# Induced-set attention with a SwiGLU network: shared load buffers and one visit of seven chunks for each attention product

## The chip, the cores and the metric

The kernel runs on one core of one Trainium2 chip. The metric is device time in microseconds (us) of one execution, the median of three runs. Engines are named as the profile names them: PE is TensorE, DVE is VectorE, ACT is ScalarE, POOL is GpSimd, SP is the sync engine, which issues the transfers.

## The reference

Four batches of 12416 tokens of 128 channels go through two attentions: 32 inducing vectors attend to the tokens, and the tokens attend to the result. What comes out (49664 tokens) goes through a gated network with 1536 hidden units.

```
def mab(q, kv):
    s = scale * (q @ kv.transpose(0, 2, 1))
    s = s - s.max(-1, keepdims=True)
    a = np.exp(s)
    a /= a.sum(-1, keepdims=True) + 1e-09
    return a @ kv
h = mab(I, x)                 # I: (4, 32, 128), x: (4, 12416, 128)
attn_out = mab(x, h)
...
g = x @ w_gate                # x: attn_out as (49664, 128)
silu = g * (1.0 / (1.0 + np.exp(-g)))
val = x @ w_val
return (silu * val @ w_out)
```

## The kernel before

**The network.** It takes nearly all of the time. The tokens of a batch make 25 columns (the code's list COLS), the hidden units 12 tiles of 128, so a batch has 300 *slots*, one for a column and a tile. In a slot the program issues, in this order of the queues:

- the *front*: two matmuls on PE, gate (L694) and value (L695), each into a PSUM buffer of the pool ps_gv. The pool has six buffers, so three pairs. The weights of this product contain the attention's result, spread over a tile called stack.
- the silu of the gate on ACT (L700), and the product of silu and value on DVE (L708). For tiles 1, 5 and 9 (DVE_TILES) the product stays in PSUM (gv); the others go into a pool of five h buffers.
- the cast of the product to h_hi on ACT (L716) and the rest h_lo on POOL, for tiles 1, 5 and 9 on DVE (both L718). Tile 11 is cast on DVE (L211). These steps, called now(w) in the code, are held back by one to three slots in a list called wait.
- the *back*: three matmuls on PE (L737, L738, L739) that add the tile's share to the output o. A back belongs to a front of 6 to 11 slots earlier; the list pend holds the fronts whose back is to come, and the number called ahead says how many it may hold. Behind the 12th back of a column DVE copies o out (L748) and SP sends it (L749).

**The attention.** It goes in *chunks*: 97 blocks of 128 tokens in seven chunks of 14 (the last 13). Batch 0's runs first, by tables of tokens (START, SECOND, FIRST). The attention of batches 1, 2 and 3 is laid into the slots of the batch before by the function plan, which gives every step a slot (add) from a dictionary of distances: PA for the *first planned batch*, PB for the *two later batches*. The main loop issues the steps that are due behind the front of the slot and ahead of its back. For one planned batch:

- load_xt brings a chunk's columns from memory into one of four buffers (xtp), load_xn its rows into one of three (xnp), both through SP.
- s1, the *scores*: matmuls of 14 blocks a chunk (L275), four chunks at one slot and three at another, seven chunks in two visits. A *visit* is a stretch in which PE leaves the network for the attention. DVE transposes the scores and takes their maximum.
- the *burst*, at one slot called e1: ACT computes all the exponentials (L307). It needs another table for this and loads silu's table back behind it. At a burst every cast that is held back goes to DVE, and ahead falls to 6, so that several backs follow at once. DVE makes a transposed tile of each chunk of exponentials, eT (L313), in a pool of four buffers.
- hacc, the *weighted sum*: matmuls of the eT tiles and the rows (L323), in three visits of three, two and two chunks, each two visits some slots apart. The first visit also sums up (h_a, L331), DVE takes the reciprocal (h_r, L335) and the normalized part (h_b); behind each later visit h_s adds that part (L344). Then h_c prepares the result.
- s2, the *second scores* of all tokens against the result: again four chunks and three (L275 too), with four more loads of columns for the first visit and the other three kept from the scores (the list S2O). DVE transposes them (L445) and takes the maximum (s2_max, L453), POOL subtracts it (s2_sub, L457).
- the second burst, e2, and then for each of six column groups: sum, reciprocal, normalization (L471, POOL), transpose to aT (L475, DVE), a_hi and a_lo (L484, POOL), and transfers to the tile stack.

A visit of steps that carry a set acc is held until the next back in pend is of none of the tiles 11, 0, 1 and 2, since it uses the PSUM buffer o between two columns.

Counted in slots of the batch that it lies in, the first planned batch has its scores at 86 and 103, the burst at 131, the weighted sums at 134, 146 and 158, the second scores at 185 and 199 and the second burst at 208. For the two later batches these are 47 and 67, 84, then 87, 96 and 102, then 127 and 138, and 149.

Of the kernel before, what the change touches and what calls it, by code (L numbers as in the profile page):

```python
# [111 lines left out]
def induced_set_attention_then_swiglu(ctx: ExitStack, tc: tile.TileContext, xt, xn, ind, wgv, wo, out):  # L112
# [103 lines left out]
    def attention(b, one, xn0=None, xt0=None):  # L216
# [88 lines left out]
        def exp1_part(q, to=None, g=0):  # L305
            sp = slice(span(q).start, span(q if to is None else to).stop)
            nc.scalar.activation(out=st.s[:, sp], in_=st.s[:, sp], func=AF.Exp, bias=st.negmax[:, g:g + 1], scale=1.0,  # L307
                                 accum_out=st.sum1[:, q:q + 1])
# [253 lines left out]
    def plan(st, p):  # L562
# [24 lines left out]
        for q in range(NXN):
            add(e1 - p["LN"][0] + p["LN"][1] * q, "load_xn", q)
            add(e1, "exp1_part", q)
            add(e1, "eT", q)  # L590
            add(e1 + p["HA"][q], "hacc", q, (0, NXN - 1))
        add(e1 + p["HA"][NXN - 1], "h_a")
        add(e1 + p["HA"][NXN - 1] + 1, "h_r")
        add(e1 + p["HA"][NXN - 1] + 1, "h_b")
        add(e1, "exp1_part", NXN, NCH - 1)
        for q in range(NXN, NCH):
            k = NXN + (q - NXN | 1)
            at = e1 + p["HB"][0] + p["HB"][1] * (k - NXN)
            add(max(at - p["HC"][0] - k + q, e1 + 1 + (p["HB"][0] + p["HB"][1] if q == NCH - 1 else p["HA"][0])), "load_xn", q)
            add(at - p["HC"][1] + 1 - k + q, "eT", q)  # L600
            add(at, "hacc", q, (k - 1, k))
        add(at + 1, "h_s")
        hn = at + p["HD"]
        add(hn, "h_c")
        for i, q in enumerate(S2O):
            k = i % NXT
            at = hn + 4 + p["H2"] * (NXT - 1) if i < NXT else hn + p["H2"] * (NCH - 1)
# [261 lines left out]
```

## Time and profile before

| what | value |
|---|---|
| median of three runs | 1376.85 us (1376.74 to 1377.32) |
| the profiled execution | 1376.59 us |
| its span | 1374.8 us |
| PE busy | 1366.1 us, 99% of the span, 7459 instructions |
| ACT busy | 1245.7 us, 91% |
| DVE busy | 1195.4 us, 87% |
| POOL busy | 1179.8 us, 86% |
| transfer queue q1 | 117.90 MB, 26.3% of 16 engines |

The span is what lies between the first and the last instruction of the profiled execution. An engine's busy time is the sum of its instructions; the matmuls of PE are pipelined, so that their modelled durations overlap and starts say more than durations. The clock that PE was granted is full (a 9) in all 40 slices of the page. Three other engines are busy for 86 to 91%, so none of them has much in hand. A row of the timeline gives the start, the time, the engine, the line, the operation, output<-input with sizes, and how many were joined (x3); in square brackets stands the idle time ahead of it and who ended that.

### The profile page before, as it was taken

What the parts mean: (1) busy time and instruction counts of PE and PEld (TensorE: products, weight loads), DVE (VectorE), ACT (ScalarE), POOL (GpSimd) and SP (SyncE); (2) the same over time, 40 slices, a digit from 0 to 9 for tenths busy, and PEclk for the clock granted to TensorE, in tenths of its full rate; (3) what the DMA queues carried; (4) which work ended last, traced back from release to release, by engine and by line L of the source; (5) the groups of instructions that cost most, each with busy time, mean ns of one, the idle gap of its engine ahead of it and who ended that gap; (6) DMA issues with size and microseconds to landing.
All of it is one profiled execution on the core that took longest, in us unless ns stands there. A gap on an engine that the chain in (4) does not pass through costs nothing.

```text
span 1374.8 us, 25215 instructions
## 1 busy us (share of the span) xinstructions
PE 1366.1 (99%) x7459; PEld 1183.8 (86%) x7459; DVE 1195.4 (87%) x2088; ACT 1245.7 (91%) x2380; POOL 1179.8 (86%) x994
## 2 busy tenths in 40 slices
PE   9999999999999999999999999999999999999998
PEld 6578788889988887899998888789999888889998
DVE  6899879998988889898898888988888888888887
ACT  4989898889998887999999889799999999999998
POOL 1689878989988878899899878889989989989987
PEclk9999999999999999999999999999999999999999
DMA  9234433312144243221123522321111111111110
GB/s 370 81 96 133 160 104 114 119 56 71 38 130 160 94 143 112 67 62 37 44 72 119 192 80 95 123 73 52 44 38 45 39 47 39 39 46 38 43 44 22
DMA packets 50680, 119.49 MB, mean 87 GB/s; under 512 B 11376, under 2 KB 28272, under 8 KB 50544
## 3 DMA queue, kind: packets, MB, share of 16 engines
q1 hardware_dynamic: 50544, 117.90, 26.3%
q8 instruction: 59, 0.97, 0.3%
q14 instruction: 77, 0.63, 0.2%
HBM read 62.54 MB, written 25.43 MB: 64 GB/s over the span
## 4 chain that ended last, share of the span: by engine, by line
PE 97%; ACT 1%; DMA 1%; DVE 1%; issue 0%; SPq 0%; DVEq 0%
PE o L737 18%; PE gv L694 18%; PE gv L695 18%; PE o L738 18%; PE o L739 18%; PE gv L275 2%; PE o L323 1%; PE o L275 1%; DMA xt_sb<-xt 1%; PE o L734 0%; ACT silu L700 0%; PE gv L424 0%; PE gv L267 0%; ACT xn_sb L184 0%; DVE eT L313 0%
## 5 line engine op out<-in xcount | busy, mean ns | idle before, releaser
L718 POOL TENSOR_TENSOR h_lo<-h,h_hi 128x512 fp32r<-128x512 f32 (+1 forms) x889 | 1088.6, 1250 | 147.7 <-ACT h_hi L716 104.7
L700 ACT ACTIVATE silu<-gv 128x512 f32<-128x512 f32 (+1 forms) x1200 | 704.8, 589 | 95.5 <-PE gv L694 69.9
L708 DVE TENSOR_TENSOR h<-gv,silu 128x512 f32<-128x512 f32 (+1 forms) x891 | 590.9, 669 | 90.5 <-PE o L738 50.7
L716 ACT CAST h_hi<-h 128x512 fp32r<-128x512 f32 (+1 forms) x778 | 468.9, 603 | 0.8 <-DVE h L708 0.8
L694 PE MATMUL gv<-stack,tw 128*128 128x512 f32 (+1 forms) x1200 | 452.7, 377 | 1.3 <-DVE stack L544 1.0
L695 PE MATMUL gv<-stack,tw 128*128 128x512 f32 (+1 forms) x1200 | 448.2, 374 | 0.0
L737 PE MATMUL o<-h_hi,wo_lo 128*128 128x512 f32 (+1 forms) x1188 | 445.6, 375 | 0.0
L739 PE MATMUL o<-h_lo,wo_hi 128*128 128x512 f32 (+1 forms) x1188 | 443.2, 373 | 0.0
L738 PE MATMUL o<-h_hi,wo_hi 128*128 128x512 f32 (+1 forms) x1188 | 443.2, 373 | 0.0
L708 DVE TENSOR_TENSOR gv<-gv,silu 128x512 f32<-128x512 f32 (+1 forms) x297 | 201.5, 678 | 66.0 <-PE o L738 46.0
L694 PEld LDWEIGHTS gv<-stack,tw 128*128 128x128 f32 x1200 | 227.0, 189 | 33.9 <-ACT tw L416 3.0
L737 PEld LDWEIGHTS o<-h_hi,wo_lo 128*128 128x128 f32 x1188 | 224.8, 189 | 33.4 <-issue 10.6
L695 PEld LDWEIGHTS gv<-stack,tw 128*128 128x128 f32 x1200 | 227.0, 189 | 28.0 <-ACT silu L700 1.6
L739 PEld LDWEIGHTS o<-h_lo,wo_hi 128*128 128x128 f32 x1188 | 224.8, 189 | 24.3 <-POOL h_lo L718 0.3
L738 PEld LDWEIGHTS o<-h_hi,wo_hi 128*128 128x128 f32 x1188 | 224.8, 189 | 23.2
L718 DVE TENSOR_TENSOR h_lo<-gv,h_hi 128x512 fp32r<-128x512 f32 (+1 forms) x297 | 197.6, 665 | 0.8
L716 ACT CAST h_hi<-gv 128x512 fp32r<-128x512 f32 (+1 forms) x295 | 168.8, 572 | 10.1 <-DVE gv L708 8.4
L211 DVE TENSOR_REDUCE h_hi<-h 128x512 fp32r<-128x512 f32 (+1 forms) x113 | 73.7, 661 | 0.0
L748 DVE COPY ob<-o 128x512 f32<-128x512 f32 (+1 forms) x99 | 65.8, 665 | 0.2 <-PE o L739 0.2
L484 POOL TENSOR_TENSOR a_lo<-aT,a_hi 128x480 fp32r<-128x480 f32 (+2 forms) x26 | 29.9, 1151 | 0.0
L196 POOL TENSOR_TENSOR wgv_sb<-s_all 128x512 int32<-128x512 int32 x2 | 2.9, 1487 | 28.4 <-ACT s_all L184 28.4
L471 POOL TENSOR_TENSOR s_all<-s_all,sm 128x512 f32<-128x512 f32 (+2 forms) x27 | 26.1, 966 | 0.0
(156 smaller groups left out, 480.2 us busy)
## 6 DMA issues: line engine op xcount, KB each, us to landing
xt_sb<-xt SPq DMA_DIRECT2D x32, 896.0 KB, 5.1
xn_sb<-xn SPq DMA_DIRECT2D x18, 896.0 KB, 6.1
out<-ob SPq DMA_DIRECT2D x52, 256.0 KB, 2.0
out<-ob SPq DMA_DIRECT2D x48, 240.0 KB, 2.0
stack<-a_hi SPq DMA_DIRECT2D x96, 64.0 KB, 2.0
stack<-a_lo SPq DMA_DIRECT2D x96, 64.0 KB, 2.0
stack<-a_hi SPq DMA_DIRECT2D x96, 60.0 KB, 2.0
stack<-a_lo SPq DMA_DIRECT2D x96, 60.0 KB, 2.0
```

Of the source, the lines that this page charges most:

```text
L211: nc.vector.tensor_reduce(out=out, in_=in_.unsqueeze(2), op=ALU.max, axis=AX.X)
L275: nc.tensor.matmul(out=ps[32 * j:32 * j + 32, 32 * (lo - b0):32 * (hi - b0)], lhsT=lhsT, rhs=st.xt[q][:, lo - CH0[q]:hi - CH0[q], j, :], s ...
L694: nc.tensor.matmul(out=u.g[:, :n], lhsT=st.w[:, wcol(0, t)], rhs=rhs, start=True, stop=True)
L695: nc.tensor.matmul(out=u.v[:, :n], lhsT=st.w[:, wcol(1, t)], rhs=rhs, start=True, stop=True)
L700: nc.scalar.activation(out=u.s[:, :u.n], in_=u.g[:, :u.n], func=AF.Silu)
L708: nc.vector.tensor_mul(out=u.h[:, :n], in0=u.v[:, :n], in1=u.s[:, :n])
L716: u.cast(out=u.hi[:, :n], in_=u.h[:, :n])
L718: eng.tensor_sub(out=u.lo[:, :n], in0=u.h[:, :n], in1=u.hi[:, :n].bitcast(F32))
L737: nc.tensor.matmul(out=o[:, :n], lhsT=wo_lo[:, ws], rhs=hi, start=(t == 0), stop=False)
L738: nc.tensor.matmul(out=o[:, :n], lhsT=wo_hi[:, ws], rhs=hi, start=False, stop=False)
L739: nc.tensor.matmul(out=o[:, :n], lhsT=wo_hi[:, ws], rhs=lo, start=False, stop=(t == NT - 1))
L748: (nc.scalar.copy if u.last else nc.vector.tensor_copy)(out=ob[:, :n], in_=o[:, :n])
```

## The change

For the planned batches both pools of load buffers serve both kinds of load: chunks 0 to 3 use the four buffers of xtp, chunks 4 to 6 the three of xnp, for columns and for rows, one after the other. So each kind of load can have all seven chunks in place, and scores, weighted sums and second scores become one visit of seven chunks each. The columns are loaded twice for all chunks (14 loads a batch instead of 10). The partial sums h_s are gone, and h_b is done once. The four instructions of the burst take other groups of chunks (EXPS). Four eT tiles are made at the burst, the other three at the weighted sum's slot, in turn with its matmuls. At the slots of scores and second scores the held tiles of DVE_TILES are finished first. The PSUM buffer rule (acc), the ramps and everything of the network are as before. Lines of the kernel after the change are a few off: L686 and L687 are the front, L692 silu, L700 the product, L710 h_lo, L729 to L731 the back.

In slots, the first planned batch now has its scores at 103, the burst at 131, the weighted sum at 134, the second scores at 170 and the second burst at 191. The two later batches: 67, 87, planned 90 and by the acc rule at 93, then 115 and 141.

```diff
-S2O = list(range(NCH - NXT, NCH)) + list(range(NCH - NXT))
 NXN = 3
+EXPS = [(0, 0), (1, 1), (2, 3), (4, 6)]
+NET = 4
...
-PA = dict(LX=(51, 5), S1=(61, 7), MX=7, E1=21, LN=(27, 4), HA=(3, 3, 3), HB=(9, 6), HC=(11, 4), HD=5, H2=6, E2=5, PR=(0, 3), PQ=2)
-PB = dict(LX=(0, 9), S1=(25, 7), MX=6, E1=11, LN=(28, 4), HA=(3, 3, 3), HB=(9, 3), HC=(10, 4), HD=6, H2=5, E2=7, PR=(0, 3), PQ=1)
+PA = dict(LX=(51, 5), S1=103, MX=7, E1=21, LN=3, HA=3, HD=5, LS=4, S2=6, E2=5, PR=(0, 3), PQ=2)
+PB = dict(LX=(0, 9), S1=67, MX=6, E1=14, LN=3, HA=3, HD=6, LS=3, S2=6, E2=5, PR=(0, 3), PQ=1)
...
-                else:
-                    st.xt[q] = xtp.tile([P, max(CH), NG, 32], F32, name="xt_sb")
+                elif xn0 is not None or q < NXT:
+                    st.xt[q] = xtp.tile([P, max(CH), NG, 32], F32, name="xt_sb")
+                else:
+                    st.xt[q] = xnp.tile([P, max(CH), C], F32, name="xn_sb").rearrange("p i (j r) -> p i j r", r=32)
...
-                if xn0 is None or q < NXN:
+                if xn0 is None and q < NXT:
+                    t = xtp.tile([P, max(CH), NG, 32], F32, name="xt_sb").rearrange("p i j r -> p i (j r)")
+                elif xn0 is None or q < NXN:
                     t = xnp.tile([P, max(CH), C], F32, name="xn_sb")
...
-            if q == group[1] and 0 < group[0] < NXN + 1:
-                h_s()
...
-        def h_s():
-            nc.vector.scalar_tensor_tensor(out=st.hn, in0=st.hps[:, 0:C], scalar=st.r, in1=st.hn, op0=ALU.mult, op1=ALU.add)
...
-            add(v1 if q < NXT else last, "s1", q, q not in (0, NXT))
...
+            add(p["LX"][0] + p["LX"][1] * q, "load_xt", q)
+            add(v1, "s1", q, q != 0)
...
+        for q in range(NCH):
+            add(v1 + 1 + p["LN"] * q, "load_xn", q)
+        for i, (q, to) in enumerate(EXPS):
+            add(e1, "exp1_part", q, to, 0, i)
+        va = e1 + p["HA"]
+        for q in range(NCH):
+            add(e1 if q < NET else va, "eT", q)
+            if q >= NET - 1:
+                add(va, "hacc", q - NET + 1, (0, NCH - 1))
+        for q in range(NCH - NET + 1, NCH):
+            add(va, "hacc", q, (0, NCH - 1))
+        add(va, "h_a"), add(va, "h_r"), add(va, "h_b")
+        add(va + p["HD"], "h_c")
+        for q in range(NCH):
+            add(va + 1 + p["LS"] * q, "load_xt", q)
+        v2 = va + 1 + p["LS"] * (NCH - 1) + p["S2"]
+        for q in range(NCH):
+            add(v2, "s2", *blocks(q), q != 0)
+            add(v2 + 1 + 2 * q, "s2_max", *blocks(q))
+            add(v2 + 3 + 3 * q, "s2_sub", *blocks(q))
+        e2 = v2 + 3 + 3 * (NCH - 1) + p["E2"]
...
-                    if step == "h_s":
+                    if step == "h_b":
                         a.hb = slot
+                    if step in ("s1", "s2"):
+                        for w in [w for w in wait if w.t in DVE_TILES]:
+                            now(w)
```

How the order of the queues moves is shown at three places.

**First place**: DVE's queue at the burst of the first planned batch and behind it. h_hi rows are the casts that the burst gives to DVE, s_all holds the exponentials, L708 (after: L700) are the value products, and the row of r is h_r's first, which follows the weighted sum's visit. Before:

```order
L211 TENSOR_REDUCE h_hi<-h 128x512 x3
L313 STREAM_TRANSPOSE eT<-s_all 128x448 x3
L708 TENSOR_TENSOR h<-gv,silu 128x512
L708 TENSOR_TENSOR gv<-gv,silu 128x512
L708 TENSOR_TENSOR h<-gv,silu 128x512
L718 TENSOR_TENSOR h_lo<-gv,h_hi 128x512
L708 TENSOR_TENSOR h<-gv,silu 128x512
L335 TENSOR_REDUCE r_2893<-gv 128x1
```

After:

```order
L212 TENSOR_REDUCE h_hi<-h 128x512 x3
L319 STREAM_TRANSPOSE eT<-s_all 128x448 x4
L700 TENSOR_TENSOR h<-gv,silu 128x512
L700 TENSOR_TENSOR gv<-gv,silu 128x512
L700 TENSOR_TENSOR h<-gv,silu 128x512
L710 TENSOR_TENSOR h_lo<-gv,h_hi 128x512
L319 STREAM_TRANSPOSE eT<-s_all 128x448 x2
L319 STREAM_TRANSPOSE eT<-s_all 128x416
L339 TENSOR_REDUCE r_2949<-gv 128x1
```

Transposes 4 to 6, which belong to the same visit, now stand behind the products of three fronts and one h_lo; the product of a fourth front, which stood ahead of h_r, has moved behind it.

**Second place**: the burst of the second planned batch. Before, on PE, the last fronts (L694, L695) and backs (L737 to L739) ahead of the weighted sum's first visit (L323), which follows the third front behind the burst:

```order
L694 MATMUL gv<-stack,tw 128x512
L695 MATMUL gv<-stack,tw 128x512
L737 MATMUL o<-h_hi,wo_lo 128x512
L738 MATMUL o<-h_hi,wo_hi 128x512
L739 MATMUL o<-h_lo,wo_hi 128x512
L694 MATMUL gv<-stack,tw 128x512
L695 MATMUL gv<-stack,tw 128x512
L323 MATMUL o<-xn_sb,eT 32x128 x42
L331 MATMUL gv<-sum_6924,fold 128x4
```

After, DVE's queue from the burst's transposes to those of the visit; each L700 is the product of one front, L740 the copy of an output:

```order
L319 STREAM_TRANSPOSE eT<-s_all 128x448 x4
L700 TENSOR_TENSOR h<-gv,silu 128x512
L700 TENSOR_TENSOR gv<-gv,silu 128x512
L740 COPY ob<-o 128x512
L700 TENSOR_TENSOR h<-gv,silu 128x512
L710 TENSOR_TENSOR h_lo<-gv,h_hi 128x512
L700 TENSOR_TENSOR h<-gv,silu 128x512 x2
L700 TENSOR_TENSOR gv<-gv,silu 128x512
L319 STREAM_TRANSPOSE eT<-s_all 128x448 x2
L319 STREAM_TRANSPOSE eT<-s_all 128x416
```

Six fronts now stand between the burst and the visit instead of three.

**Third place**: DVE's queue behind the second scores of the second planned batch. s_all<-o and s_all<-gv are the transposes of scores, mx2a and mx2b the maxima, aT and a_hi steps of a column group. Before, behind the second of the two visits:

```order
L445 STREAM_TRANSPOSE s_all<-o 128x448
L445 STREAM_TRANSPOSE s_all<-gv 128x448 x2
L445 STREAM_TRANSPOSE s_all<-gv 128x416
L708 TENSOR_TENSOR h<-gv,silu 128x512
L475 STREAM_TRANSPOSE aT<-s_all 128x480
L453 TENSOR_REDUCE mx2a<-s_all 128x14
L708 TENSOR_TENSOR gv<-gv,silu 128x512
L211 TENSOR_REDUCE a_hi<-aT 128x480
L708 TENSOR_TENSOR h<-gv,silu 128x512
L718 TENSOR_TENSOR h_lo<-gv,h_hi 128x512
L453 TENSOR_REDUCE mx2a<-s_all 128x14
L748 COPY ob<-o 128x512
```

After, behind the only one:

```order
L446 STREAM_TRANSPOSE s_all<-o 128x448
L446 STREAM_TRANSPOSE s_all<-gv 128x448 x5
L446 STREAM_TRANSPOSE s_all<-gv 128x416
L700 TENSOR_TENSOR h<-gv,silu 128x512
L454 TENSOR_REDUCE mx2a<-s_all 128x14
L700 TENSOR_TENSOR gv<-gv,silu 128x512
L740 COPY ob<-o 128x512
L700 TENSOR_TENSOR h<-gv,silu 128x512
L710 TENSOR_TENSOR h_lo<-gv,h_hi 128x512
L454 TENSOR_REDUCE mx2a<-s_all 128x14
L700 TENSOR_TENSOR h<-gv,silu 128x512 x2
L454 TENSOR_REDUCE mx2b<-s_all 128x14
```

Seven transposes and seven maxima stand behind one visit, where four and three stood behind each of two.

More of the change, by code (lines that the diff above doesn't have):

```diff
@@ L118, in induced_set_attention_then_swiglu @@
     sgl = ctx.enter_context(tc.tile_pool(name="sgl", bufs=1))
-    eTp = ctx.enter_context(tc.tile_pool(name="eTp", bufs=4))
+    eTp = ctx.enter_context(tc.tile_pool(name="eTp", bufs=NET))
     one = ctx.enter_context(tc.tile_pool(name="one", bufs=1))
@@ L303, in max_b, with exp1_part @@
             nc.vector.tensor_reduce(out=st.negmax[:, g:g + 1], in_=ps[:, :n], op=ALU.max, axis=AX.X, negate=True)
-        def exp1_part(q, to=None, g=0):
+        def exp1_part(q, to=None, g=0, col=None):
+            col = q if col is None else col
             sp = slice(span(q).start, span(q if to is None else to).stop)
             nc.scalar.activation(out=st.s[:, sp], in_=st.s[:, sp], func=AF.Exp, bias=st.negmax[:, g:g + 1], scale=1.0,
-                                 accum_out=st.sum1[:, q:q + 1])
+                                 accum_out=st.sum1[:, col:col + 1])
         def eT(q):
@@ L325, in hacc @@
                     start=(tb < NG), stop=(tb >= n1 - n0 - NG))
-            if q == group[1] and 0 < group[0] < NXN + 1:
-                h_s()
         def h_a():
             st.hp = ps_gv.tile([P, 512], F32, name="gv")
-            nc.tensor.matmul(out=st.hp[:, 0:NXN + 1], lhsT=fold.rearrange("p j m -> p (j m)"), rhs=st.sum1[:, 0:NXN + 1], start=True, stop=True)
+            nc.tensor.matmul(out=st.hp[:, 0:len(EXPS)], lhsT=fold.rearrange("p j m -> p (j m)"), rhs=st.sum1[:, 0:len(EXPS)], start=True, stop=True)
         def h_r():
             st.r = att.tile([P, 1], F32, name="r1")
-            nc.vector.tensor_reduce(out=st.r, in_=st.hp[:, 0:NXN + 1], op=ALU.add, axis=AX.X)
+            nc.vector.tensor_reduce(out=st.r, in_=st.hp[:, 0:len(EXPS)], op=ALU.add, axis=AX.X)
             nc.vector.tensor_scalar(out=st.r, in0=st.r, scalar1=1e-9, scalar2=None, op0=ALU.add)
@@ L576, in blocks @@
             return CH0[q], CH0[q] + CH[q]
-        last = p["S1"][0] + p["S1"][1] * (NCH - 1)
-        v1 = last - 3 * p["S1"][1]
+        v1 = p["S1"]
         for q in range(NCH):
-            add(p["LX"][0] + p["LX"][1] * q if q < NXT else v1 + 1 + 3 * (q - NXT), "load_xt", q)
-            add(v1 if q < NXT else last, "s1", q, q not in (0, NXT))
-        mb = last + p["MX"]
-        add(last + 2, "max_a"), add(mb, "max_b")
+            add(p["LX"][0] + p["LX"][1] * q, "load_xt", q)
+            add(v1, "s1", q, q != 0)
@@ L586, in plan @@
+        mb = v1 + p["MX"]
+        add(v1 + 2, "max_a"), add(mb, "max_b")
         e1 = mb + p["E1"]
[L587 to L607, printed above, removed]
-            add(at, "s2", *blocks(q), i not in (0, NXT))
-            if i + NXT < NCH:
-                add(at + 1, "load_xt", S2O[i + NXT])
-            d = 2 if i < NXT else 1
-            add(at + 1 + d * k, "s2_max", *blocks(q))
-            add(at + 3 + (d + 1) * k, "s2_sub", *blocks(q))
```

1 line of the change is left out of this document (removed).

## The prediction

> **What bounds the kernel now.** I read the page's span and its chain of what ended last, then the timeline of PE around the visits that the change merges.
>
> ```profile
> span 1374.8 us, 25215 instructions
> PE 97%; ACT 1%; DMA 1%; DVE 1%; issue 0%; SPq 0%; DVEq 0%
> ```
>
> The chain is PE for 97% of the span. So only what changes PE's own stream counts: the matmuls, the steps between them, the waits in front of them. The timeline of PE, second planned batch: the end of the first scores visit (four chunks), then the second one (three chunks).
>
> ```profile
> 433.21 0.96 PE L275 MATMUL o<-xt_sb,indT 128*32 128x448 f32 x8
> ...
> 436.35 0.48 PE L737 MATMUL o<-h_hi,wo_lo 128*128 128x512 f32 x1
> ...
> 456.96 0.38 PE L694 MATMUL gv<-stack,tw 128*128 128x512 f32 x1
> 457.18 0.38 PE L695 MATMUL gv<-stack,tw 128*128 128x512 f32 x1
> 457.48 0.96 PE L275 MATMUL o<-xt_sb,indT 128*32 128x448 f32 x8
> ...
> 459.82 0.48 PE L694 MATMUL gv<-stack,tw 128*128 128x512 f32 x1
> 460.14 0.38 PE L695 MATMUL gv<-stack,tw 128*128 128x512 f32 x1
> ```
>
> Read starts, not durations. Matmuls of the FFN follow each other every 0.22 us (456.96 to 457.18), so a slot of five takes 1.08, and PE has no slack. A visit to the attention costs more than its matmuls: its first starts 0.30 after the last L695 instead of 0.22 (0.08 lost), and behind it L695 follows L694 by 0.32 instead of 0.22 (0.10 lost). Inside, 56 blocks take 3.14 (433.21 to 436.35) and 41 blocks 2.34 (457.48 to 459.82): 0.0533 a block, and 0.15 that doesn't scale. **A visit costs 0.33 us beside its work.**
>
> **What the change takes away.** In each of three planned batches one scores visit, one second-scores visit and two weighted-sum visits go. The last kind, timeline of PE:
>
> ```profile
> 214.72 2.11 PE L323 MATMUL o<-xn_sb,eT 128*32 128x128 f32 x56
> ...
> 495.78 1.74 PE L323 MATMUL o<-xn_sb,eT 128*32 128x128 f32 x56
> 497.45 0.48 PE L694 MATMUL gv<-stack,tw 128*128 128x512 f32 x1
> ```
>
> 28 blocks in 1.67 are 1.49 of work at 0.0533, so 0.18 inside and the same 0.18 around it; I take 0.33 for all. 12 x 0.33 = 4.0 us. The visit at 214.72 took 0.37 longer than its twin at 495.78, a wait that goes with it. The two later batches also lose a little each between their two second-scores visits (the slip at 542.20, in the rows below, is the first of it): 0.2 each by my estimate, 0.4. **Gain 4.8 us.** The two L344 additions per batch leave DVE, where they hid; the exponentials keep four instructions over the same columns.
>
> **What it adds: three waits.** First, the merged weighted sum of the first planned batch, three slots behind the burst of exponentials as before. It needs seven transposed tiles and has four buffers: transposes 4 to 6 now stand in DVE's queue behind three value products and one h_lo (first place in the section on the change). All engines there:
>
> ```profile
> 196.85 1.95 DVE L313 STREAM_TRANSPOSE eT<-s_all 128x448 f32<-128x448 f32 x3 [0.19 <-ACT s_all L307]
> ...
> 200.02 2.60 PE L323 MATMUL o<-xn_sb,eT 128*32 128x128 f32 x84
> 201.19 1.08 ACT L700 ACTIVATE silu<-gv 128x512 f32<-128x512 f32 x2
> ...
> 204.62 0.69 DVE L708 TENSOR_TENSOR h<-gv,silu 128x512 f32<-128x512 f32 x1
> ```
>
> The products wait for ACT, which comes back from the burst at 201.19. So transpose 4 stands where the product of 204.62 stood; at 0.65 a transpose (1.95 for three at 196.85) it is done at 205.3. PE starts at 200.02 and has used four tiles (56 blocks) by 203.0. **PE waits 2.3 us**; tiles 5 and 6 come 0.6 apart, faster than PE's 0.75. The same wait can't arise twice: in the later batches the visit comes six slots behind the burst, and ACT has caught up.
>
> Second, that very distance. Before, a 2.6 us visit filled PE while ACT was in the burst (second place in the section on the change). Now six fronts stand between burst and visit, and gv holds three pairs:
>
> ```profile
> 483.25 0.38 PE L694 MATMUL gv<-stack,tw 128*128 128x512 f32 x1
> ...
> 485.00 1.09 ACT L700 ACTIVATE silu<-gv 128x512 f32<-128x512 f32 x2
> ...
> 486.24 0.68 DVE L708 TENSOR_TENSOR h<-gv,silu 128x512 f32<-128x512 f32 x1
> ```
>
> The third front after the burst is at 483.25. A fourth would come one slot later, at 484.33. Its first buffer is free when the first silu is done (485.00 + 0.55), its second when the first product is (near 486.24): the L695 that was due at 484.55 goes at 486.3. **1.75 us, in two batches: 3.5.** PE has backs in hand but they stand behind the front.
>
> Third, the stretch behind the merged second scores. All seven maxima (DVE) and subtractions (POOL), and the five steps of a column group, now follow one visit, with no second visit in which the engines catch up. How DVE ran there before, in the later batches:
>
> ```profile
> 534.43 0.38 PE L694 MATMUL gv<-stack,tw 128*128 128x512 f32 x1
> ...
> 535.53 0.69 DVE L708 TENSOR_TENSOR h<-gv,silu 128x512 f32<-128x512 f32 x1 [1.10 <-ACT silu L700]
> 536.14 0.67 DVE L475 STREAM_TRANSPOSE aT<-s_all 128x480 f32<-128x480 f32 x1
> 536.73 0.58 DVE L453 TENSOR_REDUCE mx2a<-s_all 128x14 f32<-128x448 f32 x1
> 537.23 0.69 DVE L708 TENSOR_TENSOR gv<-gv,silu 128x512 f32<-128x512 f32 x1
> ...
> 538.75 0.38 PE L694 MATMUL gv<-stack,tw 128*128 128x512 f32 x1
> ...
> 540.70 1.28 DVE L708 TENSOR_TENSOR h<-gv,silu 128x512 f32<-128x512 f32 x2
> ...
> 542.20 0.41 PE L695 MATMUL gv<-stack,tw 128*128 128x512 f32 x1
> ```
>
> DVE goes back to back from 535.53: 0.60 a step, 0.5 a maximum. The product of the front of 538.75 is the second of the pair at 540.70, so 541.30: 2.55 late, and three fronts on, L695 at 542.20 is the first that slips (0.03). So PE stops once a product starts over 2.55 behind its front. In the changed order (third place) I count from the first product after the visit to the 17th, slot 17 of the visit: 16 products, 4 h_lo, 2 output copies, 1 cast, and sum, transpose and a_hi of the column group make 26 steps of 0.6 = 15.6; 7 maxima 3.6; two small ones 0.25: 19.4. It starts 1.1 + 19.4 = 20.5 after the first front; PE reaches that front after 15 slots of 1.08 and one doubled front of 0.43, at 16.6. 3.9 late, 1.35 over. In the first batch three maxima come at once, but slots are 1.01: the same count gives 1.1 to 1.4. **1.3 us three times: 4.0.**
>
> **Loads.** Twelve more of 0.9 MB; the last of a batch is issued six slots before its visit and is the seventh chunk there, so 6.5 + 4.5 = 11 us cover it:
>
> ```profile
> xt_sb<-xt SPq DMA_DIRECT2D x32, 896.0 KB, 5.1
> ```
>
> Taken as nothing; uncovered, a visit would wait up to 5 us. On SP the first load now stands waiting for the sum to release a buffer, up to 5 us, and stack pieces queue behind it; they are issued two columns (21 slots) ahead of their use.
>
> **Sum.** -4.8 + 2.3 + 3.5 + 4.0 = **+5.0 us**. The span of 1374.8 lies in an execution of 1376.59, 0.26 under the median of 1376.85, so 1381.8.
>
> **Rivals.**
> Only the third wait is hidden: DVE's lag is real, but buffers may be handed out so that a front waits for an older product. For it: the first product of the pair at 540.70 was 3.0 late and delayed nothing. Against: the next one did. Then +1.0: 1377.8.
> A front can run two slots further than I think, in the burst too: the second and third wait both go, 2.3 remains, -2.5: 1374.3, **not slower**. It decides at five free pairs instead of three; against it stands the pool of six buffers, two a slot.
> POOL adds rather than overlaps:
>
> ```profile
> 538.51 0.94 POOL L457 TENSOR_TENSOR s_all<-s_all,mx2a 128x448 f32<-128x448 f32 x1
> 540.87 1.21 POOL L484 TENSOR_TENSOR a_lo<-aT,a_hi 128x480 fp32r<-128x480 f32 x1
> ...
> 545.98 2.53 POOL L718 TENSOR_TENSOR h_lo<-h,h_hi 128x512 fp32r<-128x512 f32 x2
> ```
>
> Sixteen h_lo at 1.26, seven subtractions at 0.94 and two steps of about 1.1 are 29 us for some 24 us of slots; five h buffers absorb half. That is 1.3 to 1.5 late at the end of the stretch, beside DVE's in my sum, but 4.2 more if the two add up: 1386.0.
> The clock drops in the stops. At the start PE's matmuls came slowly, later fast:
>
> ```profile
> 1.81 2.18 PE L646 MATMUL gv<-ident 128*128 128x128 f32 x9 [1.81 <-POOL ident masks.py:199]
> ...
> 9.43 1.75 PE L267 MATMUL gv<-ident,xt_sb 128*128 128x128 f32 x14
> ...
> 36.80 0.48 PE L694 MATMUL gv<-stack,tw 128*128 128x512 f32 x1 [1.02 <-DVE stack L544]
> 37.12 0.38 PE L695 MATMUL gv<-stack,tw 128*128 128x512 f32 x1
> 37.34 0.39 PE L413 MATMUL gv<-tw,below 128*128 128x512 f32 x1
> ```
>
> 0.24 each against 0.125, and the slow pace lasted till about 7 us: some 2.5 us lost. If each of six stops cost that, +15: 1396.8. Against: behind the 1.02 us stop at 36.80 the step is 0.22 at once, and my longest is 2.3. The Trainium skill, TensorE: Matmul & The Clock Gate, section "What's actually happening", says that PE's clock is halved by default and again after an idle window of about 3.4 us. By that rule none of the stops drops it unless two run together, and these rows agree.
>
> **How the numbers follow.** Forecast 0.46. Third wait hidden 0.20. Both gv waits hidden 0.20, of which 0.13 fall below 1374.1. POOL on top 0.11. Clock 0.03. About 0.2% (2.75 us) is what a measurement here tells from no change: faster 0.13; same 0.07 + 0.20 = 0.27; slower 0.46 + 0.11 + 0.03 = 0.60. The range goes from 1372.5, near where the gain of 4.8 comes alone, to just past the POOL case, 1386.5; the last stop's size is the least known, so it takes in the whole of the not-slower case and leaves out the clock, the POOL case's upper part and half of what lies below 1374.1.
>
> **What would show it.** PE's 97 blocks in the first planned batch should break after 56, for 2 us, with DVE's transpose as what ended it. In the later two the fourth front after the burst should wait for silu and product, and L695s should slip some 10 to 17 slots behind the second scores. Everywhere else PE should step at 0.22, with 12 visits fewer. If PE runs on without a stop at any of the three places, that term is wrong; if scores wait on xt loads, my cover of 11 us is.

## The result and the profile after

| | before | after |
|---|---|---|
| median | 1376.80 us, 4 runs (1376.65 to 1377.32) | 1385.42 us, 4 runs (1384.20 to 1386.63) |
| the profiled execution | 1376.59 us | 1386.08 us |
| its span | 1374.8 us | 1384.3 us |

The ratio is 1.0061, with a 95% interval of 1.0047 to 1.0075: slower by 8.6 us, where 5.0 was forecast with a range of 1372.5 to 1386.5. Unlike those of before, the runs after lie in two pairs: 1384.20 and 1384.76, whose mean granted clock is 1.000, and 1386.08 and 1386.63, with 0.999. The profiled execution is one of the upper pair.

The page of the changed kernel, span and chain:

```profile
span 1384.3 us, 25204 instructions
...
PE 93%; ACT 3%; DVE 2%; issue 1%; DMA 1%; SPq 0%; POOL 0%; DVEq 0%; ACTq 0%
```

PE had 97% of the chain before and has 93% now; what it lost went to ACT, DVE and "issue" (time in which an engine waited for nothing that the profile shows). The view of waits names them (engine, tile and line, whom it waited for: us in total, times, longest):

```profile
PE gv L686 <- ACT silu L692: 3.7, 5, 1.3
PE o L329 <- DVE eT L319: 1.9, 1, 1.9
```

These two kinds make 5.6 us of stops, and neither had a counterpart before. To place the whole difference I compared the start of the same front (L694 before, L686 after) in both timelines, at slots where both kernels have done the same work:

| front of | before | after | difference | what lies between |
|---|---|---|---|---|
| first planned batch, slot 80 | 131.24 | 131.68 | 0.44 | start, which the change doesn't touch |
| slot 105 | 164.09 | 164.23 | 0.14 | scores: -0.30 |
| slot 168 | 239.91 | 243.27 | 3.36 | weighted sums: +3.22 |
| slot 212 | 294.40 | 299.23 | 4.83 | second scores: +1.47 |
| next batch, slot 80 | 473.10 | 477.77 | 4.67 | scores: -0.16 |
| slot 113 | 515.60 | 521.64 | 6.04 | weighted sums: +1.37 |
| slot 140 | 550.22 | 557.22 | 7.00 | second scores: +0.96 |
| last planned batch, slot 80 | 808.09 | 814.83 | 6.74 | scores: -0.26 |
| slot 140 | 885.21 | 894.26 | 9.05 | weighted sums and second scores: +2.31 |

8.6 us lie between slot 80 and the end of the last visits. Behind the last front follow 0.45 more in this execution, which I can't place.

**The weighted sum of the first planned batch.** The timeline at the place that the prediction named:

```profile
200.16 3.26 PE L329 MATMUL o<-xt_sb,eT 128*32 128x128 f32 x112
...
204.08 0.68 DVE L710 TENSOR_TENSOR h_lo<-gv,h_hi 128x512 fp32r<-128x512 f32 x1
204.68 1.66 DVE L319 STREAM_TRANSPOSE eT<-s_all 128x448 f32<-128x448 f32 x3
205.37 3.69 PE L329 MATMUL o<-xn_sb,eT 128*32 128x128 f32 x82 [1.95 <-DVE eT L319]
208.99 0.59 PE L335 MATMUL gv<-sum,fold 128*128 128x4 f32 x2
209.44 0.77 PE L729 MATMUL o<-h_hi,wo_lo 128*128 128x512 f32 x1
210.00 0.43 PE L730 MATMUL o<-h_hi,wo_hi 128*128 128x512 f32 x1
```

56 blocks run, then PE stands for 1.95 us, until the transpose that waited behind the three products and the h_lo is done. So far the forecast. (Read by starts, as the prediction does: from the first block to the 57th it takes 5.21 here and 3.08 in e1_inplace below, which doesn't stop, so the stop costs 2.1.) But the other 41 blocks, 2.2 us of work at 0.0533, take 3.61 (205.37 to 208.99), though all transposes are done at 206.3; and the back at 209.44 shows 0.77 instead of 0.38. The same stretch in windows (the columns are the stretch, its length, the busy time with counts of PE, PEld, DVE, ACT and POOL, where PEld is PE's loading of weights, then the granted clock, the share of the transfers, GB/s):

```profile
203.00:205.30 2.30, 0.42 (x16) 0.15 (x8) 2.13 (x5) 0.92 (x2) 0.00 (x0) 1.00 0.81 327
205.30:206.70 1.40, 1.33 (x48) 1.33 (x52) 1.03 (x3) 0.00 (x0) 0.00 (x0) 0.99 0.00 0
206.70:210.00 3.30, 3.30 (x45) 2.79 (x38) 0.32 (x3) 0.00 (x0) 0.00 (x0) 0.50 0.02 5
210.00:214.00 4.00, 4.00 (x20) 3.51 (x19) 2.54 (x6) 3.10 (x6) 1.92 (x2) 0.99 0.00 0
```

PE's clock halves at 206.7, 1.3 us after PE had gone on, and stays halved for 3.4 us. That costs about 1.8: 1.4 inside the visit and 0.4 behind it. The two pairs of runs lie 1.9 apart (their middles, 1384.48 and 1386.36): the size of one such stretch.

**The burst of the later batches.** Timeline of PE, ACT and DVE at the fourth front behind the burst:

```profile
492.16 0.38 PE L731 MATMUL o<-h_lo,wo_hi 128*128 128x512 f32 x1
493.81 0.48 PE L686 MATMUL gv<-stack,tw 128*128 128x512 f32 x1 [1.28 <-ACT silu L692]
494.30 0.19 PEld L687 LDWEIGHTS gv<-stack,tw 128*128 128x128 f32 x1 [0.30 <-ACT silu L692]
494.30 0.48 PE L687 MATMUL gv<-stack,tw 128*128 128x512 f32 x1
...
491.87 1.28 ACT L692 ACT_TABLE_LOAD   x1
493.16 1.09 ACT L692 ACTIVATE silu<-gv 128x512 f32<-128x512 f32 x2
...
493.85 0.69 DVE L700 TENSOR_TENSOR h<-gv,silu 128x512 f32<-128x512 f32 x1 [1.96 <-issue]
```

The gate's matmul goes at 493.81, when the first silu since the burst has freed its buffer, and the value's at 494.30, when the second silu has ended (493.16 + 1.09 = 494.25). The value's matmul did not wait for the first product, which was still running (493.85 + 0.69 = 494.54): gates and values share the six buffers without fixed places (by the semaphores of this trace 715 of the 1200 value matmuls wait for ACT alone and 438 for DVE alone). 1.65 instead of 0.22 from the last L731, 0.49 instead of 0.22 between the two, 0.1 behind: 1.8 us, the same in the other batch.

**Behind the second scores.** PE and DVE of the second planned batch, 12 slots and more behind the visit:

```profile
542.73 0.38 PE L686 MATMUL gv<-stack,tw 128*128 128x512 f32 x1
543.04 0.48 PE L687 MATMUL gv<-stack,tw 128*128 128x512 f32 x1
...
543.79 0.38 PE L731 MATMUL o<-h_lo,wo_hi 128*128 128x512 f32 x1
544.17 0.48 PE L686 MATMUL gv<-stack,tw 128*128 128x512 f32 x1
544.70 0.48 PE L687 MATMUL gv<-stack,tw 128*128 128x512 f32 x1
...
540.81 0.65 DVE L208 TENSOR_REDUCE pairs<-s_all 128x15 f32<-128x480 f32 x1
541.49 0.18 DVE L209 TENSOR_REDUCE sm<-pairs 128x15 f32<-128x30 f32 x1
541.60 0.69 DVE L700 TENSOR_TENSOR h<-gv,silu 128x512 f32<-128x512 f32 x1
542.21 0.24 DVE L468 RECIPROCAL sm<-sm 128x15 f32<-128x15 f32 x1
542.37 0.56 DVE L454 TENSOR_REDUCE mx2a<-s_all 128x14 f32<-128x448 f32 x1
542.85 0.68 DVE L700 TENSOR_TENSOR gv<-gv,silu 128x512 f32<-128x512 f32 x1
543.44 0.68 DVE L700 TENSOR_TENSOR h<-gv,silu 128x512 f32<-128x512 f32 x1
```

DVE has no idle time in any row, and steps of 0.31, 0.38 and 0.53 on PE stand where 0.22 should.

### The profile page after: what moved, and what is told of

It reads as the page before. It is cut to its first block, busy times and chain, and to the rows that moved or that the text cites. A ratio compares the mean times of both kernels' runs of the same rounds, so it can differ in the third digit from the quotient of the medians.

```text
span 1384.3 us, 25204 instructions
## 1 busy us (share of the span) xinstructions
PE 1368.7 (99%) x7459; PEld 1184.0 (86%) x7459; DVE 1197.3 (86%) x2083; ACT 1241.5 (90%) x2379; POOL 1179.3 (85%) x994
## 4 chain that ended last, share of the span: by engine, by line
PE 93%; ACT 3%; DVE 2%; issue 1%; DMA 1%; SPq 0%; POOL 0%; DVEq 0%; ACTq 0%
PE gv L686 18%; PE gv L687 18%; PE o L729 17%; PE o L730 17%; PE o L731 17%; PE gv L280 2%; ACT silu L692 1%; PE o L329 1%; DMA xt_sb<-xt 1%; DVE h L700 1%; PE o L726 0%; ACT h_hi L708 0%; PE o L280 0%; ACT s_all L313 0%; PE gv L425 0%
## 5 line engine op out<-in xcount | busy, mean ns | idle before, releaser
L710 POOL TENSOR_TENSOR h_lo<-h,h_hi 128x512 fp32r<-128x512 f32 (+1 forms) x889 | 1088.3, 1253 | 152.8 <-ACT h_hi L708 114.7
L692 ACT ACTIVATE silu<-gv 128x512 f32<-128x512 f32 (+1 forms) x1200 | 706.5, 590 | 106.7 <-PE gv L686 84.4
L700 DVE TENSOR_TENSOR h<-gv,silu 128x512 f32<-128x512 f32 (+1 forms) x891 | 590.9, 669 | 92.5 <-PE o L730 54.1
L708 ACT CAST h_hi<-h 128x512 fp32r<-128x512 f32 (+1 forms) x777 | 469.6, 605 | 0.8 <-DVE h L700 0.8
L686 PE MATMUL gv<-stack,tw 128*128 128x512 f32 (+1 forms) x1200 | 453.1, 378 | 5.0 <-ACT silu L692 3.7
L687 PE MATMUL gv<-stack,tw 128*128 128x512 f32 (+1 forms) x1200 | 449.3, 374 | 0.4 <-ACT silu L692 0.2
L729 PE MATMUL o<-h_hi,wo_lo 128*128 128x512 f32 (+1 forms) x1188 | 444.8, 374 | 0.0
L731 PE MATMUL o<-h_lo,wo_hi 128*128 128x512 f32 (+1 forms) x1188 | 442.9, 373 | 0.0
L686 PEld LDWEIGHTS gv<-stack,tw 128*128 128x128 f32 x1200 | 226.7, 189 | 39.9 <-ACT silu L692 7.0
L700 DVE TENSOR_TENSOR gv<-gv,silu 128x512 f32<-128x512 f32 (+1 forms) x297 | 201.6, 679 | 61.7 <-PE o L730 46.8
L687 PEld LDWEIGHTS gv<-stack,tw 128*128 128x128 f32 x1200 | 226.7, 189 | 32.0 <-ACT silu L692 5.3
L729 PEld LDWEIGHTS o<-h_hi,wo_lo 128*128 128x128 f32 x1188 | 224.7, 189 | 30.0 <-issue 7.1
L731 PEld LDWEIGHTS o<-h_lo,wo_hi 128*128 128x128 f32 x1188 | 224.6, 189 | 24.5 <-POOL h_lo L710 0.3
L710 DVE TENSOR_TENSOR h_lo<-gv,h_hi 128x512 fp32r<-128x512 f32 (+1 forms) x297 | 197.5, 665 | 0.6
L708 ACT CAST h_hi<-gv 128x512 fp32r<-128x512 f32 (+1 forms) x295 | 168.9, 573 | 11.9 <-DVE gv L700 10.7
L740 DVE COPY ob<-o 128x512 f32<-128x512 f32 (+1 forms) x99 | 65.8, 665 | 0.0
```

What stands on the lines that cost most here:

```text
L686: nc.tensor.matmul(out=u.g[:, :n], lhsT=st.w[:, wcol(0, t)], rhs=rhs, start=True, stop=True)
L687: nc.tensor.matmul(out=u.v[:, :n], lhsT=st.w[:, wcol(1, t)], rhs=rhs, start=True, stop=True)
L692: nc.scalar.activation(out=u.s[:, :u.n], in_=u.g[:, :u.n], func=AF.Silu)
L700: nc.vector.tensor_mul(out=u.h[:, :n], in0=u.v[:, :n], in1=u.s[:, :n])
L708: u.cast(out=u.hi[:, :n], in_=u.h[:, :n])
L710: eng.tensor_sub(out=u.lo[:, :n], in0=u.h[:, :n], in1=u.hi[:, :n].bitcast(F32))
```

## The experiments

Each kernel was timed beside the kernel before; what counts is the distance to it.

| run | what it is | median us | before, beside it | ratio (95%) |
|---|---|---|---|---|
| after | the change itself | 1385.42 | 1376.80 | 1.0061 (1.0047 to 1.0075) |
| e1_inplace | all transposes at the burst | 1382.57 | 1377.37 | 1.0038 (1.0025 to 1.0050) |
| e2_early | later visits three fronts behind the burst | 1385.14 | 1377.37 | 1.0054 (1.0040 to 1.0068) |
| e3_both | both | 1376.96 | 1377.37 | 0.9999 (0.9990 to 1.0007) |
| e4_spread | the change, maxima every three slots | 1384.35 | 1377.37 | 1.0048 (1.0036 to 1.0061) |
| e5_split | e3_both, second scores in two visits | 1375.47 | 1377.35 | 0.9982 (0.9973 to 0.9991) |
| e6_spread4 | e3_both, maxima and subtractions every four | 1376.92 | 1377.35 | 0.9997 (0.9988 to 1.0005) |
| e7_nonow | e3_both without the rule for held tiles | 1376.91 | 1377.35 | 0.9999 (0.9990 to 1.0008) |
| e8_nosub | e3_both without subtractions | 1376.28 | 1377.13 | 0.9992 (0.9983 to 1.0001) |
| e9_onemax | e3_both with one maximum of seven | 1379.75 | 1377.13 | 1.0016 (1.0007 to 1.0025) |
| e10_none | both left out | 1373.26 | 1377.13 | 0.9972 (0.9963 to 0.9981) |
| e11_onemax | e9_onemax again | 1379.71 | 1377.10 | 1.0017 (1.0007 to 1.0027) |

### The wait for the fifth transpose: e1_inplace

```diff
-NET = 4
+NET = 7
...
-    eTp = ctx.enter_context(tc.tile_pool(name="eTp", bufs=NET))
+    eTp = ctx.enter_context(tc.tile_pool(name="eTp", bufs=4))
...
-            t = eTp.tile([P, W], F32, name="eT")
+            t = st.s[:, span(q)]
             st.eT[q] = t
-            nc.vector.transpose(out=t[:, :32 * CH[q]], in_=st.s[:, span(q)])
+            nc.vector.transpose(out=t, in_=t)
```

> All seven transposes stand at the burst, each in place in s_all, so no transpose stands behind the value products. If PE's stop in the first planned batch is the wait for the fifth eT tile (1.95 us) and the half clock behind it (about 1.8 us, in the runs whose granted clock was 0.999) follows from that stop, both go: every run at full clock, 1382.3, and the runs no more than 0.8 apart. If the stop has another cause (row loads, buffers), time and the two levels of runs stay: 1384.2 to 1386.6. If only the stop goes but the clock drops for another reason, 1382 and 1384 are both seen.

Its five runs lie between 1382.33 and 1382.77: one level. Timeline of the same visit, and the last transposes:

```profile
200.25 3.27 PE L329 MATMUL o<-xt_sb,s_all 128*32 128x128 f32 x112
203.33 2.56 PE L329 MATMUL o<-xn_sb,s_all 128*32 128x128 f32 x82
...
200.13 1.67 DVE L319 STREAM_TRANSPOSE s_all<-s_all 128x448 f32<-128x448 f32 x3 [0.20 <-ACT s_all L313]
202.10 0.69 DVE L700 TENSOR_TENSOR h<-gv,silu 128x512 f32<-128x512 f32 x1 [0.30 <-issue]
```

PE runs through all 97 blocks, and the three transposes fit into the time in which DVE waited for ACT. Stop, half clock and the second level of runs went together, as the theory had it. (The profiled execution has a mean clock of 0.999 too, but there the half clock comes at 1379.43 only, behind PE's last matmul, and costs nothing.)

### The burst of the later batches: e2_early and e3_both

e2_early is the change with the second edit alone, e3_both has this edit and that of e1_inplace.

```diff
-PB = dict(LX=(0, 9), S1=67, MX=6, E1=14, LN=3, HA=3, HD=6, LS=3, S2=6, E2=5, PR=(0, 3), PQ=1)
+PB = dict(LX=(0, 9), S1=67, MX=6, E1=11, LN=2, HA=3, HD=6, LS=3, S2=6, E2=5, PR=(0, 3), PQ=1)
```

> In the two later batches the burst is three slots earlier and row loads come every two slots, so that the weighted sum stands three fronts behind the burst as in the kernel before; four eT tiles as in the change. If PE's stop of 1.8 us at the fourth front behind the burst is the wait for a gv pair, it goes in both batches (-4.0 with its small followers), and the wait for the fifth eT tile comes in its place, 2.05 each, and half clock behind each stop in some runs, 0 to 1.8: 1384.3 without any drop, up to 1390 with three. If the stop is only moved or is of another kind, it stays beside the eT wait: 1388 and more.

> Both edits together. If the two stops are what they are taken for, neither is left: 1385.4 - 2.05 - 0.9 (half of the runs had 1.8 of half clock) - 4.0 = 1378.4, at full clock in every run. If one takes the place of the other, 1380.5 to 1382.5.

In e2_early the gv stop is gone and the wait for the transpose stands in all three batches. Timeline of PE, second halves of the three visits:

```profile
205.44 2.59 PE L329 MATMUL o<-xn_sb,eT 128*32 128x128 f32 x82 [1.95 <-DVE eT L319]
...
492.58 3.73 PE L329 MATMUL o<-xn_sb,eT 128*32 128x128 f32 x82 [2.60 <-DVE eT L319]
...
830.87 2.59 PE L329 MATMUL o<-xn_sb,eT 128*32 128x128 f32 x82 [1.90 <-DVE eT L319]
```

and its windows behind these stops:

```profile
205.40:210.00 4.60, 4.56 (x92) 4.17 (x93) 1.83 (x6) 0.65 (x2) 0.00 (x0) 1.00 0.03 8
...
494.20:497.60 3.40, 3.40 (x41) 2.84 (x32) 0.62 (x4) 0.00 (x0) 0.00 (x0) 0.55 0.02 5
...
830.80:836.00 5.20, 5.13 (x95) 4.67 (x96) 2.40 (x8) 1.22 (x3) 0.04 (x1) 1.00 0.02 3
```

In this execution the clock halved behind the stop of 2.60 us only. The stop of 1.95 in the first planned batch, the same as in the change, left it full here and halved it there. So such a stop may or may not cost 1.8 more (the last section compares the stretches); the five runs spread from 1383.30 to 1386.25.

e3_both has neither stop: 1376.96, 1.4 below what was expected (2.0 by the distance to the kernel before), and no different from the kernel before. That leaves the stops behind the second scores as what eats the gain.

### Behind the second scores: e4_spread, e5_split, e6_spread4

e4_spread, on the change:

```diff
-            add(v2 + 1 + 2 * q, "s2_max", *blocks(q))
+            add(v2 + 1 + 3 * q, "s2_max", *blocks(q))
```

> The seven maxima behind the second scores come every three slots instead of every two, nothing else. If the stops some 12 to 21 slots behind that visit (1.5 us a batch) come from DVE falling behind, 0.8 to 1.3 of each goes: 1381.5 to 1383 as the median, with the two levels of the clock still there. If POOL sets them, or silu on ACT by itself, nothing changes: 1385.4.

7.0 above before instead of 8.6: between what the two theories gave it, and its runs (1382.88 to 1385.12) overlap with those of the change, so the time alone is inconclusive. The starts of fronts in its profile say more. Between slots 113 and 140 of the later batches, where the change loses 0.96, it loses 0.10 each, and 0.2 more behind; between 168 and 212 of the first planned batch it loses 1.47, as the change does. So in two of three batches the pace of the maxima moves the stops.

e5_split, on e3_both:

```diff
-            add(v2, "s2", *blocks(q), q != 0)
-            add(v2 + 1 + 2 * q, "s2_max", *blocks(q))
-            add(v2 + 3 + 3 * q, "s2_sub", *blocks(q))
+            h, k = (0, q) if q < NXT else (12, q - NXT)
+            add(v2 + h, "s2", *blocks(q), k != 0)
+            add(v2 + h + 1 + 2 * k, "s2_max", *blocks(q))
+            add(v2 + h + 3 + 3 * k, "s2_sub", *blocks(q))
```

> On top of e3_both, only the second scores go back to two visits of four and three chunks, 12 slots apart; scores and weighted sums stay one visit. In e3_both's profile PE stops for 1.5 us behind the second scores in the first planned batch and 1.15 in each later one. If these stops are DVE's backlog of seven maxima without a visit to catch up in, the split takes most of it away and costs 0.33 three times: 1377.0 - 3.8 + 1.0 + 0.4 = 1374.6. If the stops come from something the split leaves (the burst's distance, POOL's subtractions, the column group's steps), only the price of the visits is seen: 1378.0.

1.9 below before, so 1.5 below e3_both, where 2.4 was expected: the split pays for its three visits and more, and PE's waits show no stop behind the second scores. It is the only version with the whole computation that is faster than the kernel before, by 0.18% (0.09 to 0.27%).

e6_spread4, on e3_both:

```diff
-            add(v2 + 1 + 2 * q, "s2_max", *blocks(q))
-            add(v2 + 3 + 3 * q, "s2_sub", *blocks(q))
-        e2 = v2 + 3 + 3 * (NCH - 1) + p["E2"]
+            add(v2 + 1 + 4 * q, "s2_max", *blocks(q))
+            add(v2 + 3 + 4 * q, "s2_sub", *blocks(q))
+        e2 = v2 + 3 + 4 * (NCH - 1) + p["E2"]
...
-PA = dict(LX=(51, 5), S1=103, MX=7, E1=21, LN=3, HA=3, HD=5, LS=4, S2=6, E2=5, PR=(0, 3), PQ=2)
+PA = dict(LX=(51, 5), S1=103, MX=7, E1=21, LN=3, HA=3, HD=5, LS=4, S2=11, E2=5, PR=(0, 3), PQ=2)
```

> On top of e3_both, the one visit of second scores stays, but maxima and subtractions follow every four slots instead of every two and three, the second burst is six slots later, and in the first planned batch the visit is planned where it was issued (slot 170), so that no three maxima come at once. If the backlog is what stops PE, 2.5 to 3.8 goes without the price of a visit: 1373.2 to 1374.5. If the stops don't depend on the pace of the maxima, 1377.0.

1376.92: nothing gained. The stops come later. Its timeline of DVE shows why:

```profile
548.30 0.69 DVE L700 TENSOR_TENSOR h<-gv,silu 128x512 f32<-128x512 f32 x1 [0.64 <-POOL h_lo L710]
...
552.91 0.69 DVE L700 TENSOR_TENSOR h<-gv,silu 128x512 f32<-128x512 f32 x1 [1.04 <-POOL h_lo L710]
```

and a window of it:

```profile
530.00:546.00 16.00, 15.94 (x74) 13.37 (x73) 15.80 (x29) 14.18 (x28) 16.00 (x15) 1.00 0.15 46
```

Of 16 us DVE (third busy time) works 15.80 and POOL (the fifth) all 16.00. Slower maxima leave DVE's backlog smaller for a while, but then a product waits for an h buffer that POOL has not yet read. Two engines are full here, not one. Since this version changes the pace of the subtractions and the second burst too, it doesn't tell which of the two holds PE.

### Which of the two engines: e8_nosub, e9_onemax, e10_none, e11_onemax

e8_nosub, on e3_both; it leaves out the subtraction of the maximum in the planned batches:

```diff
-            add(v2 + 3 + 3 * q, "s2_sub", *blocks(q))
```

e9_onemax, on e3_both; all chunks of a planned batch take the first chunk's maximum:

```diff
-            add(v2 + 1 + 2 * q, "s2_max", *blocks(q))
+            if q == 0:
+                add(v2 + 1, "s2_max", *blocks(q))
...
-            eng.tensor_sub(out=sl2(b0, b1), in0=sl2(b0, b1), in1=st.mx2[b0][:, :n].unsqueeze(2).broadcast_to([P, n, M]))
+            eng.tensor_sub(out=sl2(b0, b1), in0=sl2(b0, b1), in1=st.mx2.get(b0, st.mx2.get(0))[:, :n].unsqueeze(2).broadcast_to([P, n, M]))
```

e10_none has both edits, and so takes one maximum and subtracts nothing in the planned batches.

> On top of e3_both, the planned batches leave out the seven subtractions of the maximum (POOL, 6.6 us a batch); the maxima stay. In e6_spread4's profile DVE and POOL were both busy all the time between 530 and 546 us, and two of DVE's products waited for h buffers that POOL held. Stops of 3.8 us in all are to be had. If POOL's load is the bound behind the second scores: 1373.2. If DVE's is: 1377.0. If each is by itself: 1375 to 1376.5.

> On top of e3_both, the planned batches take one maximum for the whole batch of second scores, that of the first chunk, instead of seven (DVE, 3.1 us a batch less); the subtractions stay. If DVE's load is the bound: 1373.2. If POOL's is: 1377.0. If each is by itself: 1375 to 1376.5.

> Both left out: six of seven maxima and all subtractions. Every theory of the two engines expects the stops to go: 1373.2. If a stop of more than 0.5 us a batch stays, something else holds PE behind the second scores, and 1375 or more is seen.

e10_none came out as expected, 3.9 below before and so 3.5 below e3_both (0.4 below): nothing but the load of DVE and POOL holds PE there. e8_nosub, 0.85 below before, gained only 0.4 on e3_both. Timeline of PE, first e3_both and then e8_nosub, the first stop behind the second scores:

```profile
537.20 0.42 PE L686 MATMUL gv<-stack,tw 128*128 128x512 f32 x1
537.82 0.48 PE L687 MATMUL gv<-stack,tw 128*128 128x512 f32 x1 [0.20 <-ACT silu L692]
...
539.00 0.48 PE L686 MATMUL gv<-stack,tw 128*128 128x512 f32 x1
```

```profile
536.36 0.42 PE L685 MATMUL gv<-stack,tw 128*128 128x512 f32 x1
536.99 0.48 PE L686 MATMUL gv<-stack,tw 128*128 128x512 f32 x1 [0.20 <-ACT silu L691]
...
538.16 0.48 PE L685 MATMUL gv<-stack,tw 128*128 128x512 f32 x1
```

With 6.6 us less on POOL, the stop is the same to 0.01 us (0.62 and 1.18 against 0.63 and 1.17). So it isn't POOL's; it is DVE's backlog. What e8_nosub gained lies at the second burst, where e3_both has one step of 0.44 to 0.47 in each batch and e8_nosub none.

e9_onemax was to take just that backlog away, and stood 2.6 above before, 3.0 above e3_both. One of its executions, the profiled one, took 8259.56 us, with every matmul at some 1.67 us instead of 0.37, so that its profile shows none of these waits. The same kernel once more:

> The kernel of e9_onemax once more: its profiled execution there took six times as long in every matmul, so that nothing could be read from it, and its other runs stood at 1378.5 to 1380.4, above e3_both, which no theory expected. If that chip's state was the reason, 1373.9 to 1376.5 comes now (DVE's share of the stops gone). If it repeats, 1379.5, the profile must show a stop of about 0.9 in each batch that e3_both has not, where POOL's subtractions, no longer waiting for maxima, stand ahead of h_lo.

It repeats: 1379.71. One further execution took 6937.21 us; nothing here explains those two, and no other kernel of this study had one. The waits of PE and of DVE in the undisturbed profile:

```profile
PE gv L425 <- DVE h L701: 2.9, 2, 1.4
...
DVE h L701 <- POOL h_lo L711: 14.2, 25, 1.7
```

The stops of DVE's backlog are gone. In the first planned batch others stand in their place: a product waits 1.68 for POOL at 263.58, and PE stops for buffers that products hold, 0.9 of it at 268.5 ahead of the burst. Over that batch the loss is the same: from slot 80 to slot 80 of the next batch 0.32 against the kernel before, and 0.28 in e3_both. In each later batch PE stops behind the second burst: the first matmuls that spread the result (L425) need a gv buffer that a product holds, and that product waits for POOL. Timeline of PE and DVE there, first e11_onemax and then e3_both:

```profile
550.71 0.85 PE L425 MATMUL gv<-wgv_sb,hT 128*32 128x384 f32 x8 [1.43 <-DVE h L701]
...
549.96 0.69 DVE L701 TENSOR_TENSOR h<-gv,silu 128x512 f32<-128x512 f32 x1 [1.71 <-POOL h_lo L711]
```

```profile
549.34 1.50 PE L425 MATMUL gv<-wgv_sb,hT 128*32 128x384 f32 x16
...
550.45 0.69 DVE L700 TENSOR_TENSOR h<-gv,silu 128x512 f32<-128x512 f32 x1 [1.72 <-POOL h_lo L710]
```

The same product waits for POOL as long in e3_both, and there PE passes without a stop. By the trace's semaphores the second half of L425 waits for DVE in e11_onemax and for ACT in e3_both: it was given a buffer that a product still holds instead of one that a silu had long freed. (In e10_none it waits for DVE too and passes, since there POOL has less to do.) So this stop is not a larger backlog of POOL; the edit changed which buffer the step gets. It explains why relief of DVE alone ends above e3_both: by the starts of fronts, e11_onemax loses nothing on it in the first planned batch and 0.9 in each later one, 1.8 in this execution, the fastest of its runs. The rest of the 3.0 I can't place. What relief of DVE alone is worth with the buffers as in e3_both, no run here shows. Shown are: with POOL relieved, DVE's stops stay; with both relieved, no stop is left.

### The rule for held tiles: e7_nonow

On e3_both:

```diff
-                    if step in ("s1", "s2"):
-                        for w in [w for w in wait if w.t in DVE_TILES]:
-                            now(w)
```

> On top of e3_both, the rule that finishes the held tiles of DVE_TILES at a visit's slot is left out. My theory gives it no part in the result: 1377.0, within 0.5. The rival, that the rule gains by giving DVE something to do ahead of the visit, gives 1377.6 to 1378.5.

1376.91 beside 1376.96: the rule has no part in e3_both's time.

## Why the prediction was right, and where its sizes were off

The sign was right, and three waits stood where the prediction put them. The first had the releaser that it named, DVE's transpose. In the second the gate's matmul had it too, the first silu, but the value's waited for the second silu and not for the first product. In the third both matmuls of a front waited for silu, which waited for DVE. e1_inplace took the first wait away; e2_early took the second away and brought the first into the later batches instead; e3_both has neither and stands 9.0 lower against the kernel before than the change, where 7.0 was expected. Some 0.7 of the difference is that the stops behind the second scores are smaller there (1.15 instead of 1.5 in the later batches).

The size was short by 3.6 of 8.6 us. As an estimate from the table of fronts: 0.9 is the half clock (1.8 in two of four runs), 0.9 the start and the end of the profiled execution, and the other 1.8 the sizes of the gain and of the waits. That 1385.4 lies within the range is in part luck: it stands nearer to the case of POOL on top (1386.0), which did not happen, than to the forecast (1381.8), and the half clock, which did, was not in the range's account.

- **The gain of 4.8.** The three scores visits gave 0.30, 0.16 and 0.26, where 0.33 was put; behind the longer visit DVE is a little late in the later batches (at 469.93 silu waits 0.23 for a product, and PE slips by 0.16). e10_none, which has no stops left in these stretches and sheds some work besides, stands 3.9 under the kernel before. So 4.8 was somewhat too much.
- **The first wait, 2.3.** It was 2.1 by starts (1.95 in the view of waits). The step that failed is the one on the clock: "behind the 1.02 us stop at 36.80 the step is 0.22 at once, and my longest is 2.3" was taken as proof that no stop of mine halves the clock. A stop of 1.95 did, in the profiled execution; the two pairs of runs say that it did in two of four. 1.8 us in half of the runs are 0.9 in the median. The rival was priced at six drops and 15 us, with a chance of 0.03; one drop in every second run was never among the cases. The Trainium skill, TensorE: Matmul & The Clock Gate, section "What's actually happening", has the clock halve after an idle window of about 3.4 us and says that the window runs freely. The drops agree with a free-running window: in the traces' record of the clock each lasts 3.413 us, and it begins 201.386 us after the clock was first granted in full here and 488.106 us in e2_early, which are 59 and 143 times 3.413. They do not agree with 3.4 us of idleness: stops of 1.95 and 2.60 were enough.
- **The second wait, 1.75 twice.** 1.8 twice, as put, though by another way for the value's matmul, and 0.2 of small slips behind it. Three fronts between burst and visit, as before the change, remove it (e2_early, e3_both).
- **The third wait, 1.3 three times.** It was about 1.8 in the first planned batch (1.47 net, with 0.33 for the visit) and 1.5 in the later ones (0.96 net, with 0.33 and the 0.2 that went). The mechanism was DVE's backlog, as said. But it stopped PE from the 11th front behind the visit on in the first planned batch and the 13th in the later ones, not the 17th, and the gate's matmul was stopped too (262.05, 0.38 for silu), not only the value's. The prediction left out the link through ACT: with two silu buffers (the first number of BF) silu waits for the product of two fronts earlier, 0.90 at 264.33.
- **The rival of POOL.** "4.2 more if the two add up" did not happen: without subtractions (e8_nosub) DVE's stops are unchanged. That was tested on e3_both and not on the change. POOL holds products of its own accord (1.72 at 550.45 in e3_both), as the prediction had it beside DVE's lag; whether PE stops for that hangs on which buffer comes next.
- **Loads at nothing.** Right: PE's waits show no load in a planned batch.

Of the rest, the start is 0.44 later and the end 0.45 in this execution; the start isn't the change's (its first front comes at 36.8 to 38.2 in the profiles of this study), for the end it stays open.

## What to carry to other kernels

A visit to other work is also a rest for the engines behind the busiest one: before merging visits, count in which of them DVE, ACT or POOL caught up, and whether PE can stand their backlog through the buffers there are. Of such merges, take those whose followers fit, and keep the split where a batch of small steps hangs on the visit: scores and weighted sums in one visit, with all transposes at the burst, and second scores in two, is 0.18% faster than the kernel before. When two engines are both nearly full, as here, easing one can show little, or less than nothing; ease both in one run before dropping the theory. And compare what the steps behind the edit wait for in both kernels: an edit can change which buffer a step is given, and the stop that comes of it looks like a new bound.

## What was not expected of the hardware

A stop of PE of 1.95 us can halve its clock, though not each time, and it does so 1.3 us after PE has gone on, for 3.41 us (206.68 to 210.09). Cut into stretches of 3.413 us that are in step with the clock's own changes, the executions with the wait for the transpose give (PE's busy time by the profile's modelled ends of matmuls):

| stretch | PE busy of 3.41 us | granted clock in the next stretch |
|---|---|---|
| e2_early, 490.44 to 493.85 | 1.27 | 0.50 |
| after, 203.26 to 206.68 | 1.47 | 0.50 |
| e4_spread, 204.55 to 207.96 | 1.47 | 1.00 |
| e2_early, 828.36 to 831.77 | 1.51 | 1.00 |
| e2_early, 203.72 to 207.13 | 1.69 | 1.00 |

So a stop of 1.95 that a boundary cuts in two (the last row) left the clock full, and one that lies within a stretch stands just at the edge: 1.47 dropped it once and once not. Five stretches are few, and what decides at the edge is open. Stops of 1.28 by the view of waits, which the change and e1_inplace have twice per execution, show no second level of times in e1_inplace's runs (1382.33 to 1382.77). And a transpose of 128x448 in place, output over input, took 0.62 us in the mean (24 of them), as one into another tile does.
